# Reordering the warm-up half of an mLSTM + squared-ReLU FFN kernel: early sigmoids, rounding words ahead of exponentials, squares behind num, evenly spread rounding steps

## Chip, cores, metric

One core of one Trainium2 chip. The metric is device time of one execution in microseconds (us), median over several runs. Each run also reports the span of the core (first to last instruction) and the mean clock that TensorE was granted (1.000 is full).

In the text PE is TensorE (matmul), DVE is VectorE, ACT is ScalarE, POOL is GpSimd.

## The reference

```python
# attention part: q,k,v,o_gate (4, 8, 768, 40), i_gate,f_gate (4, 8, 768), all float32
for t in range(S):
    m_new = max(f[t] + m, i[t]);  f_s = exp(f[t] + m - m_new);  i_s = exp(i[t] - m_new);  m = m_new
    C = f_s * C + i_s * outer(v[t], k[t]);   n = f_s * n + i_s * k[t]
    y[t] = sigmoid(o_gate[t]) * (C @ q[t]) / max(|n . q[t]|, 1)
# bridge to x (3072, 320); FFN with w_in (320, 2048), w_out (2048, 320)
out = maximum(x @ w_in, 0)**2 @ w_out
```

The kernel does the recurrence in 24 chunks of 128 steps. The weights arrive as 64-bit words and are rounded to float32 on the chip in 26 pieces.

Of the kernel before, what the change touches and what calls it, by code (L numbers as in the profile page):

```python
# [9 lines left out]
F32 = mybir.dt.float32  # L10
# [3 lines left out]
AF = mybir.ActivationFunctionType  # L14
# [3 lines left out]
P = 128  # L18
# [11 lines left out]
def kernel(  # L30
# [25 lines left out]
    nc = tc.nc  # L56
# [39 lines left out]
    ident = consts.tile([P, P], F32)  # L96
# [158 lines left out]
    st = {}  # L255
# [14 lines left out]
    def load_o(s):  # L270
        b, c = divmod(s, NB)
        r, (s0, s1) = next((r, (a, z)) for r, (a, z) in enumerate(RUNS) if a <= s < z)
        if s == s0:
            st["og", r] = ld.tile([P, 4, H, D], F32, name="og")
        og = st.setdefault(s, {})["og"] = st["og", r][:, s - s0]
        nc.sync.dma_start(og, o_gate[b, :, c * P : (c + 1) * P, :].rearrange("h p d -> p h d"))

    def sigmoid(s):
        nc.scalar.activation(st[s]["og"], st[s]["og"], AF.Sigmoid)

    def load_A(s):
        b, c = divmod(s, NB)
        d = st.setdefault(s, {})
        A = ld.tile([P, H, P], F32, name="A_bc", bufs=2)
        d["A"] = [A]
        nc.sync.dma_start(
            A[:], bass.AP(A_d.tensor, A_d.offset + b * H * S + c * P, [[0, P], [S, H], [1, P]]),
        )
# [19 lines left out]
    def mask(s):  # L308

        A = st[s]["A"][0]  # L310
        nc.gpsimd.affine_select(  # L311
            A[:], A[:], compare_op=ALU.is_ge, fill=-1e30, base=0, pattern=[[0, H], [1, P]], channel_multiplier=-1,
        )

    def weigh(s, masked=False):
        b, c = divmod(s, NB)
        d = st[s]
        A, n = d["A"], H // len(d["A"])
        d["W"] = prep.tile([P, H, P], F32, name="W_sb")
        d["dec"] = prep.tile([P, H], F32, name="dec")  # L320
        if len(A) == 1 and not masked:
            mask(s)
        for i in range(len(A)):
            hh = slice(i * n, (i + 1) * n)
            for h in range(n):
                nc.scalar.activation(  # L326
                    d["W"][:, i * n + h, :], A[i][:, h, :], AF.Exp, bias=b_T[:, b, c, i * n + h : i * n + h + 1],
                )
            nc.scalar.activation(d["dec"][:, hh], A[i][:, :, P - 1], AF.Exp)
        values(s)  # L330
# [37 lines left out]
    def weighted(s, spare=False):  # L368
        d = st[s]
        d["P"] = []  # L370
        for i in range(2):
            t = ffn.tile([P, W], F32, name="r_sb", bufs=4) if spare else work.tile([P, W], F32, name="P_sb")
            t = t[:].rearrange("p (j t) -> p j t", j=PR)
            d["P"].append(t)
            nc.vector.tensor_tensor(  # L375
                t, d["sc"][i], d["W"][:].rearrange("p (j two) t -> p j two t", two=2)[:, :, i, :], op=ALU.mult,
            )

    def attend(s):
        b, c = divmod(s, NB)  # L380
        d = st[s]
        C = st.get("C")
        if c > 0:
            hi = ps_at.tile([P, H, D1], F32, name="hi", tag="at")
            for j in range(PR):
                nc.tensor.matmul(  # L386
                    hi[:, 2 * j : 2 * j + 2, :].rearrange("p h d -> p (h d)"), lhsT=d["qT"][:, j, :],
                    rhs=C[:, j].rearrange("p h d -> p (h d)"), start=True, stop=True,
                )
        if c + 1 < NB:  # L390
            dC = ps_at.tile([P, PR, 2, D1], F32, name="dC", tag="at")
            for j in range(PR):
                nc.tensor.matmul(  # L393
                    dC[:, j].rearrange("p h d -> p (h d)"),
                    lhsT=d["kq"][:, 0, 2 * j : 2 * j + 2, :].rearrange("p h d -> p (h d)"),
                    rhs=d["vw"][:, 2 * j : 2 * j + 2, :].rearrange("p h d -> p (h d)"), start=True, stop=True,
                )
        hp = d["hp"] = ps_at.tile([P, H, D1], F32, name="hp", tag="at")
        for h in range(H):
            nc.tensor.matmul(  # L400
                hp[:, h, :], lhsT=d["P"][h % 2][:, h // 2, :], rhs=d["va"][:, h, :], start=True, stop=True,
            )
        d["num"] = hp
        if c > 0:
            num = d["num"] = work.tile([P, H, D1], F32, name="num", bufs=1)
            nc.vector.tensor_tensor(  # L406
                num[:], hi[:], eA_T[:, b, c, :].unsqueeze(2).to_broadcast([P, H, D1]), op=ALU.mult,
            )
        if c + 1 < NB:
            Cn = work.tile([P, PR, 2, D1], F32, name="C_sb")  # L410
            nc.vector.tensor_tensor(Cn[:], dC[:], bdm[:], op=ALU.mult)  # L411
            if c > 0:
                Cd = work.tile([P, H, D1], F32, name="Cd", bufs=1)
                nc.gpsimd.tensor_tensor(
                    Cd[:], C[:].rearrange("p j i d -> p (j i) d"),
                    d["dec"][:].unsqueeze(2).to_broadcast([P, H, D1]), op=ALU.mult,
                )
                Cf = Cn[:].rearrange("p j i d -> p (j i) d")
                nc.gpsimd.tensor_tensor(Cf, Cf, Cd[:], op=ALU.add)  # L419
            st["C"] = Cn  # L420
# [17 lines left out]
    def turn_rows(s):  # L438
        d = st[s]
        g, j = divmod(s, GT)  # L440
        if j == 0:
            st["xT", g] = xts.tile([P, 3, WG], F32, name="xT")
        tp = ps_at.tile([P, 3, P], F32, name="tp", tag="at")
        for a in range(3):
            nc.tensor.transpose(tp[:, a, :], d["x"][:, a * P : (a + 1) * P], ident[:])  # L445
        nc.scalar.copy(st["xT", g][:, :, j * P : (j + 1) * P], tp[:])
        del st[s]
# [29 lines left out]
    def ffn1(g, pp):  # L477
        ffn1_main(g, pp)
        ffn1_rest(g, pp, st["half"][0])

    def relu_half():
        if "half" in st:
            hs, g4 = st.pop("half")
            rs = []
            for h in hs:
                rs.append(ffn.tile([P, 2, WG], F32, name="r_sb", bufs=4))
                nc.scalar.activation(rs[-1][:], h[:], AF.Relu)  # L487
            st["relu"] = rs, g4

    def square_half():  # L490
        if "relu" in st:
            rs, g4 = st.pop("relu")
            for i, r in enumerate(rs):
                nc.vector.tensor_tensor(g4[:, :, i, :], r[:], r[:], op=ALU.mult)  # L494

# [122 lines left out]
    def idle(n):  # L618
        t = ps_h.tile([P, W], F32, name="idle", tag="h_ps")
        for _ in range(n):  # L620
            nc.tensor.matmul(t[:], lhsT=zeros[:, :P], rhs=zeros[:], start=True, stop=True)
# [43 lines left out]
    weighted(1, spare=True)  # L665
    load(2)
    load_A(2)
    sigmoid(0)
    sigmoid(1)
    attend(0)  # L670
    rounding.step()
    normalise(0)
    load_o(2)
    load_o(3)
    mask(2)
    attend(1)
    normalise(1)
    load(3)
    load_A(3)
    rounding.step()  # L680

    nc.scalar.activation(consts.tile([P, 1], F32, name="warm")[:], ident[:, :1], AF.Exp)
    turn_rows(0)
    idle(4)
    transposes(2)
    idle(4)
    turn_rows(1)
    weigh(2, masked=True)
    rounding.step()


    NEXT = (5, 8, 10, 11, 12, 14, 15, 17, 19, 21, 23, 26)
    assert NEXT[-1] == len(pieces)
    for u in range(8):
        s = 2 + u // 2
        relu_half()
        if u % 2 == 0:
            if u == 0:
                ffn1(0, 0)
                scores(s)  # L700
                rounding.step()
            else:
                turn_rows(s - 1)
                scores(s)
                ffn1(u // 4, u % 4)
            weighted(s)
            weigh(s + 1)
            if u == 2:
                rounding.step()
                rounding.step()  # L710
            square_half()
        else:
            load_A(s + 2)
            for r in {1: (4,), 3: (5, 6), 5: (7,), 7: ()}[u]:
                load(r)
            if u in (1, 5):
                for r in range(s, s + 2 + u // 2):
                    sigmoid(r)
            attend(s)
            rounding.join()  # L720
            normalise(s)
            for r in {5: (8,), 7: (9,)}.get(u, ()):
                load(r)
            if u > 4:
                load_o(2 * s)
                load_o(2 * s + 1)
            transposes(s + 1)
            rounding.words()
            ffn1(u // 4, u % 4)
            square_half()  # L730
        if u < 4:
            load_o(4 + u)
        while rounding.done < NEXT[u]:
            rounding.step()
# [94 lines left out]
```

## The kernel before, where the change touches it

One *piece* of weights is fetched, then `words` (two ScalarE instructions) and `join` (three on VectorE, one add on GpSimd) round it. `step` does the words of the next piece and the join of this one. In the timelines below VectorE, ScalarE and GpSimd each run their own instructions in the order in which the program lists them, so an instruction can be held up by those listed before it on its engine.

The tile names: `hi` and `hp` are the two parts of a chunk's output (from the state carried over, and from within the chunk), `dC` is the chunk's addition to the state `C_sb`, `P_sb` are the weighted scores that `hp` reads, `num` is the sum of both parts, `x_sb` the gated and normalised output. The *turns* are TensorE's transposes of `x_sb`; ScalarE copies them to `xT`, which the first FFN product (`ffn1`) reads together with `w_in`.

```python
def words(self):                                  # ScalarE x2
    nc.scalar.activation(mag[:, :w], raw[:, :, 1].bitcast(F32), AF.Abs)
    nc.scalar.activation(low[:, :w], raw[:, :, 0].bitcast(U32), AF.Copy, bias=2.0, scale=2.0 ** -51)
def join(self):                                   # VectorE x3, GpSimd x1
    nc.vector.tensor_scalar(mag, mag, ...);  nc.vector.tensor_scalar(bits, bits, ...)
    nc.vector.scalar_tensor_tensor(bits, in0=self.raws[n][:, :w, 1], ..., in1=bits, ...)
    nc.gpsimd.tensor_tensor(dst.bitcast(I32), bits, low.bitcast(I32), op=ALU.add)   # dst: w_in or w_out
    self.fetch()                                  # next raw piece, once this buffer is free
...
def weigh(s, masked=False):                       # ScalarE: 8 exponentials; GpSimd: mask, vw
    if len(A) == 1 and not masked: mask(s)        # GpSimd
    ...
def attend(s):                                    # TensorE hi, dC, hp in three PSUM banks (bufs=3)
    ...                                           # VectorE num <- hi, C_sb <- dC; GpSimd Cd, C_sb
def normalise(s):                                 # VectorE: num += hp; dm; x_sb = num * og * dm
    ...
def relu_half(): ...                              # ScalarE: r_sb (bufs=4) <- h_ps
def square_half(): ...                            # VectorE: g <- r_sb * r_sb

# first half: 8 steps u, two for each chunk s = 2..5
NEXT = (5, 8, 10, 11, 12, 14, 15, 17, 19, 21, 23, 26)     # pieces done after each step; last four later
for u in range(8):
    s = 2 + u // 2
    relu_half()
    if u % 2 == 0:
        ...                                       # turn_rows(s-1), scores(s), ffn1
        weighted(s)                               # VectorE: P_sb
        weigh(s + 1)
        if u == 2:
            rounding.step(); rounding.step()
        square_half()
    else:
        ...                                       # loads
        if u in (1, 5): ...                       # sigmoids of the coming chunks
        attend(s); rounding.join(); normalise(s)
        transposes(s + 1); rounding.words(); ffn1(u // 4, u % 4); square_half()
    while rounding.done < NEXT[u]: rounding.step()
```

## Time and profile before

| | before |
|---|---|
| time, median of the first 3 runs | 573.0 us (572.72 to 574.24) |
| profiled execution | span 575.1 us, clock 0.985 |
| busy | PE 98%, DVE 54%, ACT 34%, POOL 17% |

TensorE is nearly always busy, so look for where it is not, and where it runs at half clock. The prediction below shows the lines: three sites, A near 50 us, B near 62 us, C near 132 us.

One line that it used without showing it is VectorE's wait inside site B (timeline of VectorE, before; in brackets the idle time just before and who ended it):

```profile
58.16 0.43 DVE L194 TENSOR_SCALAR mag<-mag 128x512 f32<-128x512 f32 x1 [2.25 <-ACT mag L183]
...
60.65 2.36 DVE L494 TENSOR_TENSOR g<-r_sb 128x512 f32<-128x512 f32 x2
62.93 0.49 DVE L406 TENSOR_TENSOR num<-hi,eA_T 128x328 f32<-128x328 f32 x1
```

VectorE stands still for 2.25 us, until ScalarE has finished the exponentials and made the next magnitude; then join, squares and only then num, for which TensorE waits.

### The profile page before, as it was taken

To read this page: it belongs to the slowest core of one execution; us is meant where nothing else is said; L and a number is where in the kernel's file an instruction comes from. 1 tells how busy PE (TensorE), PEld (TensorE's weight loads), DVE (VectorE), ACT (ScalarE), POOL (GpSimd) and SP (SyncE) were. 2 spreads that over 40 slices of the span, in tenths; PEclk is the share of its full clock that TensorE was granted. 3 is DMA by queue.
4 is the path that set the end of the run, shared out by engine and by line. 5 is a ranking of instruction groups with operands and counts; after the bars stand their busy time and mean duration, and the time that the engine had idled before them with its cause. 6 is when DMAs were issued, how large, how long until landed. Compare 5 with 4: busy or idle time off the path is not lost.

```text
span 575.1 us, 9748 instructions
## 1 busy us (share of the span) xinstructions
PE 562.9 (98%) x3879; PEld 503.8 (88%) x3879; DVE 308.7 (54%) x602; ACT 195.8 (34%) x486; POOL 97.3 (17%) x113
## 2 busy tenths in 40 slices
PE   8998899999999999999999999999999999999997
PEld 5875788887789989989989988988998998988997
DVE  8687867597373364364365356246355454424441
ACT  3868376280442232423213315205126204112000
POOL 3354523233011120100211220101210210000000
PEclk9998799997999999999999999999999999999999
DMA  9996979932132432321441343141321000000000
GB/s 193 229 217 151 151 158 181 179 105 35 59 47 54 90 46 61 83 47 38 84 69 38 62 91 61 27 102 38 47 62 38 0 24 2 1 24 0 25 24 23
DMA packets 130909, 42.60 MB, mean 74 GB/s; under 512 B 101072, under 2 KB 127696, under 8 KB 130864
## 3 DMA queue, kind: packets, MB, share of 16 engines
q1 hardware_dynamic: 130768, 41.79, 35.4%
q8 instruction: 30, 0.49, 0.4%
q10 hardware_dynamic: 96, 0.20, 0.1%
q14 instruction: 15, 0.12, 0.1%
HBM read 37.95 MB, written 4.03 MB: 73 GB/s over the span
## 4 chain that ended last, share of the span: by engine, by line
PE 91%; DVE 5%; ACT 2%; issue 1%; DMA 1%; POOL 0%; SPq 0%; POOLq 0%; ACTq 0%; DVEq 0%
PE h_ps L555 30%; PE h_ps L461 28%; PE h_ps L472 7%; PE hp L400 7%; PE tp L363 4%; PE tp L350 4%; PE dC L393 3%; PE hi L386 3%; PE h_ps L501 3%; DVE mag L198 1%; PE tp L445 1%; DVE g L494 1%; DMA kq<-in_q_dram 1%; ACT W_sb L326 1%; PE A_ps L302 1%
## 5 line engine op out<-in xcount | busy, mean ns | idle before, releaser
L461 PE MATMUL h_ps<-xT,w_in 128*128 128x256 f32 x768 | 180.3, 389 | 2.7 <-POOL w_in L203 2.1
L461 PEld LDWEIGHTS h_ps<-xT,w_in 128*128 128x128 f32 x768 | 144.8, 193 | 26.7 <-issue 3.0
L487 ACT ACTIVATE r_sb<-h_ps 128x512 f32<-128x512 f32 x96 | 49.9, 602 | 176.1 <-PE h_ps L472 170.9
L494 DVE TENSOR_TENSOR g<-r_sb 128x512 f32<-128x512 f32 x96 | 61.3, 698 | 70.3 <-ACT r_sb L487 70.3
L555 PE MATMUL h_ps<-w_out,g 128*128 128x160 f32 x528 | 76.9, 302 | 0.0
L555 PEld LDWEIGHTS h_ps<-w_out,g 128*128 128x128 f32 x528 | 72.5, 190 | 1.3 <-ACT r_sb L487 0.3
L326 ACT ACTIVATE W_sb<-A_bc,b_T 128x128 f32<-128x128 f32 x176 | 53.8, 394 | 6.4 <-POOL A_bc L311 6.4
L555 PE MATMUL h_ps<-T,S 128*128 128x160 f32 x352 | 51.4, 299 | 0.0
L472 PE MATMUL h_ps<-xT,w_in 64*128 64x256 f32 x384 | 49.0, 391 | 0.0
L555 PEld LDWEIGHTS h_ps<-T,S 128*128 128x128 f32 x352 | 49.0, 190 | 0.0
L400 PE MATMUL hp<-va,P_sb 128*128 128x41 f32 x368 | 45.7, 286 | 0.0
L472 PEld LDWEIGHTS h_ps<-xT,w_in 64*128 64x128 f32 x384 | 34.8, 186 | 12.3 <-issue 9.0
L337 POOL TENSOR_TENSOR vw<-va,W_sb 128x328 f32<-128x328 f32 x20 | 16.4, 821 | 169.9 <-ACT W_sb L326 140.4
L400 PEld LDWEIGHTS hp<-va,P_sb 128*128 128x128 f32 x368 | 44.5, 198 | 0.0
L569 DVE TENSOR_TENSOR y_sb<-y_sb,h_ps 128x160 f32<-128x160 f32 x33 | 10.6, 321 | 55.1 <-PE h_ps L555 55.1
L375 DVE TENSOR_TENSOR P_sb<-tp,W_sb 128x512 f32<-128x512 f32 x46 | 29.6, 685 | 16.0 <-PE tp L363 15.5
L419 POOL TENSOR_TENSOR C_sb<-C_sb,Cd 128x328 f32<-128x328 f32 x16 | 14.1, 879 | 140.0 <-DVE C_sb L411 139.9
L569 DVE TENSOR_TENSOR y_sb<-h_ps,y_sb 128x160 f32<-128x160 f32 x22 | 7.1, 325 | 49.5 <-PE h_ps L555 30.9
L350 PE MATMUL tp<-ident,kq 128*128 128x128 f32 x192 | 26.2, 280 | 2.7 <-DVE num L406 2.4
L578 ACT COPY y_sb<-h_ps 128x160 f32<-128x160 f32 x11 | 3.2, 292 | 70.6 <-PE h_ps L555 63.9
L363 PEld LDWEIGHTS tp<-qT,kT 40*128 40x128 f32 x384 | 24.2, 187 | 3.3 <-issue 1.8
L363 PE MATMUL tp<-qT,kT 40*128 40x128 f32 x384 | 26.9, 279 | 0.0
(98 smaller groups left out, 672.1 us busy)
## 6 DMA issues: line engine op xcount, KB each, us to landing
A_bc<-a_rows SPq DMA_DIRECT2D x22, 512.0 KB, 4.3
raw<-in_moe_w_out_dram SPq DMA_DIRECT2D x16, 320.0 KB, 3.3
raw<-in_moe_w_in_dram SPq DMA_DIRECT2D x8, 512.0 KB, 5.5
kq<-in_k_dram SPq DMA_DIRECT2D x24, 160.0 KB, 4.3
kq<-in_q_dram SPq DMA_DIRECT2D x24, 160.0 KB, 4.0
va<-in_v_dram SPq DMA_DIRECT2D x24, 160.0 KB, 4.3
og<-in_o_gate_dram SPq DMA_DIRECT2D x24, 160.0 KB, 4.3
out_dram<-y_sb SPq DMA_DIRECT2D x24, 160.0 KB, 1.8
```

Of the source, the lines that this page charges most:

```text
L326: nc.scalar.activation(d["W"][:, i * n + h, :], A[i][:, h, :], AF.Exp, bias=b_T[:, b, c, i * n + h : i * n + h + 1],)
L350: nc.tensor.transpose(tp[:, j, :], d["kq"][:, i, 2 * j : 2 * j + 2, :].rearrange("p h d -> p (h d)"), ident[:],)
L363: nc.tensor.matmul(sc[i][:, j, :], lhsT=d["kT"][rows, j, :], rhs=d["qT"][rows, j, :], start=True, stop=True,)
L375: nc.vector.tensor_tensor(t, d["sc"][i], d["W"][:].rearrange("p (j two) t -> p j two t", two=2)[:, :, i, :], op=ALU.mult,)
L386: nc.tensor.matmul(hi[:, 2 * j : 2 * j + 2, :].rearrange("p h d -> p (h d)"), lhsT=d["qT"][:, j, :], rhs=C[:, j].rearrange("p h d -> p (h ...
L400: nc.tensor.matmul(hp[:, h, :], lhsT=d["P"][h % 2][:, h // 2, :], rhs=d["va"][:, h, :], start=True, stop=True,)
L461: nc.tensor.matmul(hs[i][:, n, :], lhsT=w_in[:, a, fb * P : (fb + 1) * P], rhs=xT[:, a, :], start=(n == 0 and a == 0), stop=False,)
L472: nc.tensor.matmul(hs[i][:, n, :], lhsT=w_in2[rows, 2 * pp + n, :], rhs=xT[rows, 2, :], start=False, stop=(n == 1),)
L487: nc.scalar.activation(rs[-1][:], h[:], AF.Relu)
L494: nc.vector.tensor_tensor(g4[:, :, i, :], r[:], r[:], op=ALU.mult)
L555: nc.tensor.matmul(to, lhsT=lhsT[:, p], rhs=rhs[:, p, :], start=(start and p == 0), stop=(p == NPAIR - 1), skip_group_check=True,)
L569: add = lambda to, a, b: nc.vector.tensor_tensor(to, a, b, op=ALU.add)
```

## The change

Four parts. (1) The o_gate loads and sigmoids of chunks 2 and 3 move up behind those of chunks 0 and 1, and the one-element `warm` exponential, which loaded the exp table early, is dropped. (2) In step 2 the words of piece 9 come before the exponentials, and the two joins before them too. (3) The squares of that step move into step 3, behind num. (4) `NEXT` gives the steps from the fifth on more pieces and the last one fewer.

```diff
-            st["relu"] = rs, g4
+            st.setdefault("relu", []).append((rs, g4))       # square_half pops the oldest
@@ setup
     load_A(2)
+    load_o(2)
+    load_o(3)
     sigmoid(0)
     sigmoid(1)
@@ (further down: load_o(2), load_o(3) removed)
-    nc.scalar.activation(consts.tile([P, 1], F32, name="warm")[:], ident[:, :1], AF.Exp)
     turn_rows(0)
     idle(4)
     transposes(2)
     idle(4)
+    sigmoid(2)
+    sigmoid(3)
     turn_rows(1)
     weigh(2, masked=True)
@@ steps
-    NEXT = (5, 8, 10, 11, 12, 14, 15, 17, 19, 21, 23, 26)
+    NEXT = (5, 8, 10, 11, 13, 15, 17, 19, 21, 23, 25, 26)
@@ even u
+            if u == 2:
+                rounding.words()
             weighted(s)
-            weigh(s + 1)
             if u == 2:
-                rounding.step()
-                rounding.step()
-            square_half()
+                mask(s + 1)
+                rounding.join()
+                rounding.join()
+                weigh(s + 1, masked=True)
+                rounding.words()
+            else:
+                weigh(s + 1)
+                square_half()
@@ odd u
-            if u in (1, 5):
-                for r in range(s, s + 2 + u // 2):
+            if u == 5:
+                for r in range(4, 8):
                     sigmoid(r)
             attend(s)
+            if u == 3:
+                square_half()
```

## The prediction

> **What bounds the kernel now.** I read the page first. Its parts 1 and 2 say that TensorE sets the time: 98% busy, and the granted clock is full except at the start and in three slices.
>
> ```profile
> PE 562.9 (98%) x3879; PEld 503.8 (88%) x3879; DVE 308.7 (54%) x602; ACT 195.8 (34%) x486; POOL 97.3 (17%) x113
> PE   8998899999999999999999999999999999999997
> PEclk9998799997999999999999999999999999999999
> ```
>
> A slice is 14.4 us, so the dips (8, 7, 7 tenths) lie at 43-58, 58-72 and 129-144 us. From 145 us on nothing is lost; whatever the early part gains should stay in the total. The list of waits of TensorE and its timeline name the gaps.
>
> ```profile
> PE tp L350 <- DVE num L406: 2.4, 1, 2.4
> PE h_ps L461 <- POOL w_in L203: 2.1, 1, 2.1
> PE dC L393 <- DVE P_sb L375: 1.3, 1, 1.3
> ...
> PE tp L445 <- DVE x_sb L435: 0.9, 2, 0.7
> ```
>
> In the timeline the columns are start, us, engine, line, operation:
>
> ```profile
> 51.30 4.98 PE L461 MATMUL h_ps<-xT,w_in 128*128 128x256 f32 x14 [2.08 <-POOL w_in L203]
> 63.47 1.97 PE L350 MATMUL tp<-ident,kq 128*128 128x128 f32 x8 [2.43 <-DVE num L406]
> 133.06 1.10 PE L393 MATMUL dC<-vw,kq 128*128 128x82 f32 x8 [1.35 <-DVE P_sb L375]
> 133.99 3.52 PE L400 MATMUL hp<-va,P_sb 128*128 128x41 f32 x16
> ```
>
> Each gap costs more than its length: the eight transposes after the second take 1.97 us, against 1.07 elsewhere. One-microsecond windows show why (the last columns are granted clock, DMA share and GB/s):
>
> ```profile
> 51.00:52.00 1.00, 0.70 (x3) 0.65 (x4) 0.97 (x2) 0.98 (x2) 0.25 (x1) 1.00 0.84 259
> 53.00:54.00 1.00, 1.00 (x4) 0.82 (x3) 0.97 (x3) 0.00 (x0) 1.00 (x2) 0.50 0.59 82
> ...
> 65.00:66.00 1.00, 1.00 (x5) 0.91 (x4) 0.93 (x4) 0.73 (x3) 0.30 (x1) 0.50 1.19 298
> ...
> 136.00:137.00 1.00, 1.00 (x7) 1.00 (x6) 0.00 (x0) 0.00 (x0) 0.77 (x1) 0.50 1.02 167
> ```
>
> From the fractions at the edges, the clock is half from 52.1 to 55.5 (3.4 us), 62.3 to 69.15 (6.8) and 134.0 to 140.8 (6.8). Half clock for t costs about t/2: 1.7, 3.4 and 3.4 us. So:
> - Site A (46-56 us): 0.65 + 2.08 + 1.7 = 4.4 us.
> - Site B (61-69 us): 2.43 + 3.4 = 5.8 us.
> - Site C (131-141 us): 1.35 + 3.4 = 4.8 us.
> All three: 15 us, 2.6% of 573. That is the ceiling.
>
> **What the Trainium skill says.**
> - "TensorE: Matmul & The Clock Gate", "What's actually happening": activity is judged in windows of 3413 ns, with only half or full clock. The trace agrees: 1.00 and 0.50, lengths 3.4 and 6.8. The page has the drop come after an idle window; here gaps of 1.35 to 2.43 us suffice. The 0.65 us gap at 46.3 did not.
> - "SBUF — State Buffer", "SBUF: two separate sides": VectorE and GpSimd share one port pair as an exclusive lock. The trace agrees: the x_sb product takes 1.17 us at 45.13 and ends 0.34 us after the GpSimd add that began at 44.69, against 0.44 alone.
> - "ScalarE: Activation LUTs", "What ACT_TABLE_LOAD costs": 1283 ns plus a drain of about 1380. The trace has the load at 1.28 us; the next sigmoid follows 0.01 us later, so no drain after it shows here.
>
> **The change, part by part.**
>
> *Sigmoids 2 and 3 early.* This is the view of before around them:
>
> ```profile
> 31.09 2.45 ACT L326 ACTIVATE W_sb<-A_bc,b_T 128x128 f32<-128x128 f32 x8
> 43.34 1.28 ACT L279 ACT_TABLE_LOAD   x1
> 44.63 0.83 ACT L279 ACTIVATE og<-og 128x320 f32<-128x320 f32 x2
> 45.13 1.17 DVE L434 TENSOR_TENSOR x_sb<-num,og 128x320 f32<-128x320 f32 x1 [2.79 <-ACT og L279]
> 49.94 1.31 POOL L203 TENSOR_TENSOR w_in<-mag,low 128x512 int32<-128x512 int32 x1 [3.98 <-ACT low L185]
> ```
>
> The change removes the load and sigmoids at 43.34 (2.1 us), the load at 51.19, the warm-up at 25.1, and VectorE's 2.79 us wait. The sigmoids go into ScalarE's idle time at 29.6-30.4 with their table still active. But without the warm-up the exp load now stands directly before chunk 2's exponentials: load 31.2-32.5, exponentials to 34.95, then the magnitudes that piece 4's rounding on VectorE needs at 35.6, where before they were ready at 34.2. GpSimd's vw (to 35.7) and join 3 (to 36.95) take the lock; piece 4's three VectorE steps end near 38.4 instead of 37.3. P_sb of chunk 2 stands behind them: 38.3 instead of 37.23. The first half ends near 39.0, and dC (38.07 before) needs its bank: a **new gap** of about 1.1 us at 38.
>
> After it everything is 1 us later: mask(3) 39.7, exponentials to 43.3. In before, GpSimd did vw, Cd, C and join 5 (0.74+0.74+0.88+1.27) while VectorE stood idle. Now both want the lock at 43.3-48.6: the GpSimd four (about 3.3 us net of overlap) and VectorE's two products, copy and two squares (about 2.0) alternate. x_sb is ready at 45.4 (before 47.07), so the 0.65 us gap goes; but piece 6's VectorE steps begin at 48.55 (before 48.18) and its GpSimd add ends near 51.6 (before 51.25). TensorE reaches that point at 49.1. The gap at A stays, about 2.5 us, with its half clock. **A: 0.65 + 2.08 becomes 1.1 + 2.5, some 0.4 us worse.**
>
> *Words ahead, squares behind num.* Piece 9's words now precede the exponentials, so VectorE no longer waits 2.25 us for them at 58.16: from 52.5 it runs P_sb (1.3), join 8 (2.4) and join 9 (2.5 with the lock) to 58.7. hi of chunk 3 is ready then, and num runs at 58.75-59.2 instead of 62.93. hp ends near 61.35 and the transposes follow without a wait: B's 2.43 + 3.4 us go. The squares (1.3) are moved, not dropped. They come before x_sb of chunk 3: squares with vw between 60.1-62.0, join 10 with Cd and C to 64.4, the num sum and normalisation with GpSimd's add and mask to 67.9. TensorE, after transposes 0.9 and ffn1 4.6, wants that x_sb at 66.9 and waits about 1 us. Before, it started those turns at 71.78: **71.8 - 68.0 = 3.8 us gained, A's loss and this wait included.**
>
> *Steps spread.* One step with 320 columns costs VectorE 0.32+0.33+0.49 = 1.15 us, 1.7 under the lock. The part before site C had three steps, now it has one; three steps from 127.67 to 132.3 held P_sb until 132.23:
>
> ```profile
> 125.26 2.50 DVE L494 TENSOR_TENSOR g<-r_sb 128x512 f32<-128x512 f32 x4 [0.41 <-ACT r_sb L487]
> 132.23 1.28 DVE L375 TENSOR_TENSOR P_sb<-tp,W_sb 128x512 f32<-128x512 f32 x2
> ```
>
> With one, P_sb starts relative to TensorE at about 129, before hi ends at 131.7; dC need not wait. **4.8 us gained.** The added steps fall in the stretch from 70 to 115 us, where VectorE idles 1.3 to 3.6 us at a time and TensorE never waits; I count them as free. Sum: 3.8 + 4.8 = 8.6 us. For the two new gaps near 1 us I take a chance of about one in three each that the clock halves, at about 2.5 us: 1.6 us. 573 - 8.6 + 1.6 = 566.
>
> **The rivals.**
> 1. *The new gaps are as good as the old ones.* If the exp load before chunk 2 and the late x_sb of chunk 3 both halve the clock (2 x 3.4 us), only 1.8 us is left: 571. For: 1.35 us halved it. Against: the two gaps are shorter, and 0.65 us did not.
> 2. *Site A goes as well.* If the lock alternates less badly, piece 6 lands by 49.5 as the removed wait suggests, and A loses its 2.5 + 1.7 us: 562 or a little less. For: 2.79 us of VectorE's wait do disappear. Against: GpSimd's four operations must still be done there.
> 3. *Only the spread matters*: squares shift B's wait from num to x_sb in full; then C alone gives 4.8 us, 568.
> 4. *Late gates*: if the o_gate of chunks 2 and 3 has not landed by 29.6 (issued near 22 instead of 24.39, median time to land 5.8 us), ScalarE's copy before the first ffn1 is held: up to 1 us more.
>
> **Range and chances.** The sum's best form is 562-564 and rival 1 gives 571; 8 in 10 lie in 561 to 570.5. Faster by over 2% means below 561.5: A must go too, 0.18. Slower by over 2% would need new losses of 20 us: 0.01.
>
> **What would show it right or wrong.** Right: no wait of the chunk 4 transposes on num and none of dC near 130 us, so clock 1.00 there; VectorE no longer waiting on the sigmoids; one exp load before the exponentials at 31; TensorE still waiting on GpSimd's w_in (2 to 2.8 us) near 50, and dC of chunk 2 waiting about 1 us on P_sb. Wrong: no w_in wait (the lock argument fails), half clock right after 38 or 67 us (short gaps count in full), or a new TensorE wait between 70 and 130 us (the spread steps are not free).

## The result

| | before | after |
|---|---|---|
| time, median | 573.16 us (572.72 to 574.24, 4 runs) | 568.49 us (567.82 to 569.93, 4 runs) |
| ratio | | 0.9919, 95% interval 0.9895 to 0.9943 |
| profiled execution | 575.1 us, clock 0.985 | 565.8 us, clock 0.999 |

A ratio is the mean time of one kernel's runs over that of the other's of the same rounds, so not quite the ratio of the medians. The gain is 0.8%, 4.7 us by the medians. The two profiled executions, though, lie 9.3 us apart: twice as much. Keep that in mind.

The page of the kernel after, parts 1 and 2:

```profile
PE 554.9 (98%) x3878; PEld 497.8 (88%) x3879; DVE 312.0 (55%) x602; ACT 193.1 (34%) x483; POOL 98.1 (17%) x113
PEclk9999999999999999999999999999999999999999
```

The clock is full in every slice. TensorE's waits:

```profile
PE tp L445 <- DVE x_sb L435: 3.0, 2, 2.4
PE h_ps L461 <- POOL w_in L203: 1.8, 1, 1.8
...
PE dC L393 <- DVE P_sb L375: 1.1, 1, 1.1
```

The wait of 2.4 us on num is gone. The 1.1 us for dC is not the old one: it stands near 39 us now, as the timeline of TensorE shows:

```profile
39.42 1.09 PE L393 MATMUL dC<-vw,kq 128*128 128x82 f32 x8 [1.08 <-DVE P_sb L375]
51.66 3.29 PE L461 MATMUL h_ps<-xT,w_in 128*128 128x256 f32 x14 [1.77 <-POOL w_in L203]
67.52 0.52 PE L445 MATMUL tp<-ident,x_sb 128*128 128x128 f32 x3 [2.39 <-DVE x_sb L435]
128.00 1.92 PE L400 MATMUL hp<-va,P_sb 128*128 128x41 f32 x16
```

At site C (last line) dC and hp follow without a wait and at full clock: 1.92 us for hp, 3.52 before. At A the fourteen ffn1 matmuls take 3.29 us at full clock, 4.98 before at half clock; but the wait for w_in ends at 51.66, as before (51.30). At B the turns of chunk 3 start at 67.52 instead of 71.78.

Two squares at A, which take 1.29 us together in the profile before (first line), take 1.97 after, and the x_sb product takes 0.92 us (before: 0.49), with GpSimd's vw, Cd, C and rounding add now running at the same time (43.70 to 48.67):

```profile
46.98 1.29 DVE L494 TENSOR_TENSOR g<-r_sb 128x512 f32<-128x512 f32 x2
```
```profile
44.09 0.92 DVE L435 TENSOR_TENSOR x_sb<-x_sb,dm 128x320 f32<-128x320 f32 x1
...
45.57 1.97 DVE L494 TENSOR_TENSOR g<-r_sb 128x512 f32<-128x512 f32 x2
```

VectorE in site B, after:

```profile
58.04 0.69 DVE L199 SCALAR_TENSOR_TENSOR mag<-raw,mag 128x512 int32<-128x512 int32 x1
58.65 0.49 DVE L406 TENSOR_TENSOR num<-hi,eA_T 128x328 f32<-128x328 f32 x1
...
59.47 2.38 DVE L494 TENSOR_TENSOR g<-r_sb 128x512 f32<-128x512 f32 x2
...
66.88 0.49 DVE L435 TENSOR_TENSOR x_sb<-x_sb,dm 128x320 f32<-128x320 f32 x1
```

num is 4.3 us earlier than before, while x_sb of chunk 3, the end of the same queue, is done at 67.6 instead of 68.9. The other part of the 4.3 us by which the turns moved is half clock in the profile of before: there TensorE came to the turns 2.9 us after x_sb was ready, and at full clock (gaps_filled, below) the old order reaches them at 69.43. So at full clock the change gains about 1.9 us at B (an estimate, from one profile of each). Between 31 and 67.5 us VectorE is busy 33.8 of 36.5 us (93%), TensorE 30.7. **In this stretch VectorE is taken to be the bound** (the experiments test it), though TensorE is the busiest engine of the whole span.

### The profile page after: what moved, and what is told of

It is laid out like the page before. It is cut to its first block, busy times and chain, and to the rows that moved or that the text cites. A ratio compares the mean times of both kernels' runs of the same rounds, so it can differ in the third digit from the quotient of the medians.

```text
span 565.8 us, 9740 instructions
## 1 busy us (share of the span) xinstructions
PE 554.9 (98%) x3878; PEld 497.8 (88%) x3879; DVE 312.0 (55%) x602; ACT 193.1 (34%) x483; POOL 98.1 (17%) x113
## 4 chain that ended last, share of the span: by engine, by line
PE 92%; DVE 4%; ACT 1%; issue 1%; DMA 1%; POOL 0%; POOLq 0%; SPq 0%; DVEq 0%
PE h_ps L555 30%; PE h_ps L461 28%; PE h_ps L472 8%; PE hp L400 7%; PE tp L363 4%; PE tp L350 3%; PE h_ps L501 3%; PE dC L393 3%; PE hi L386 3%; PE tp L445 1%; PE idle L621 1%; PE A_ps L302 1%; ACT W_sb L326 1%; DVE mag L198 1%; PE A_ps L298 1%
## 5 line engine op out<-in xcount | busy, mean ns | idle before, releaser
L461 PE MATMUL h_ps<-xT,w_in 128*128 128x256 f32 x768 | 176.7, 383 | 2.3 <-POOL w_in L203 1.8
L461 PEld LDWEIGHTS h_ps<-xT,w_in 128*128 128x128 f32 x768 | 142.2, 190 | 25.1 <-issue 3.0
L487 ACT ACTIVATE r_sb<-h_ps 128x512 f32<-128x512 f32 x96 | 49.9, 601 | 173.8 <-PE h_ps L472 170.6
L400 PE MATMUL hp<-va,P_sb 128*128 128x41 f32 x368 | 44.1, 280 | 0.0
L400 PEld LDWEIGHTS hp<-va,P_sb 128*128 128x128 f32 x368 | 42.9, 192 | 0.0
L446 ACT COPY xT<-tp 128x384 f32<-128x384 f32 x24 | 11.4, 477 | 43.2 <-PE tp L445 43.2
```

Of the source, the lines that this page charges most:

```text
L400: nc.tensor.matmul(hp[:, h, :], lhsT=d["P"][h % 2][:, h // 2, :], rhs=d["va"][:, h, :], start=True, stop=True,)
L461: nc.tensor.matmul(hs[i][:, n, :], lhsT=w_in[:, a, fb * P : (fb + 1) * P], rhs=xT[:, a, :], start=(n == 0 and a == 0), stop=False,)
L487: nc.scalar.activation(rs[-1][:], h[:], AF.Relu)
```

## The experiments

All are correct against the reference. Each was timed in five rounds, with runs of the kernel before beside them. Ratios are to before; where two calls used the same chip, the record pools their runs of before (13 in all for the two calls on one chip, 11 of them already in the first).

| run | median us (range) | ratio (95% interval) | profiled: span, clock |
|---|---|---|---|
| spread_undone | 570.44 (569.63-570.99) | 0.9944 (0.9917-0.9970) | 568.5, 0.993 |
| spread_alone | 571.84 (571.07-572.41) | 0.9970 (0.9943-0.9996) | 569.7, 0.991 |
| sigmoids_undone | 570.29 (567.81-572.79) | 0.9943 (0.9908-0.9978) | 566.3, 0.997 |
| sigmoids_alone | 577.17 (573.45-578.03) | 1.0046 (1.0012-1.0081) | 575.5, 0.985 |
| squares_undone | 569.65 (567.53-570.94) | 0.9918 (0.9884-0.9952) | 569.2, 0.988 |
| gaps_filled | 572.79 (571.21-573.20) | 0.9978 (0.9949-1.0007) | 569.4, 1.000 |
| squares_behind_x | 567.40 (566.51-568.91) | 0.9890 (0.9861-0.9919) | 565.4, 0.994 |
| words_before_first | 568.41 (566.09-570.00) | 0.9902 (0.9868-0.9936) | 564.2, 0.997 |
| words_undone | 572.58 (569.34-573.94) | 0.9960 (0.9921-1.0000) | 570.2, 0.990 |
| step_before_squares | 569.07 (567.27-571.14) | 0.9910 (0.9875-0.9945) | 566.9, 0.991 |
| three_together | 567.47 (564.73-568.96) | 0.9875 (0.9833-0.9917) | 565.6, 0.997 |
| after_again | 569.82 (568.85-571.47) | 0.9927 (0.9893-0.9960) | 569.7, 0.988 |

The intervals are 0.5 to 0.8% wide, that is about 1.5 to 2.4 us to either side. Differences between two runs below about 2 us are therefore not told apart by time, and I then rest on the waits in the traces.

### The spread: undone, and alone

```diff
-    NEXT = (5, 8, 10, 11, 13, 15, 17, 19, 21, 23, 25, 26)
+    NEXT = (5, 8, 10, 11, 12, 14, 15, 17, 19, 21, 23, 26)
```

> The kernel after, with the old list of rounding steps (12, 14, 15, 17, 19, 21, 23, 26). My theory (three VectorE steps held P_sb and with it dC, 1.35 us of wait, plus up to 3.4 us of half clock where the clock drops): the wait of dC on P_sb near 125 us comes back at about 1.3 us; time 1.5 to 4.8 us over the 568.5 of the kernel after, so 570 to 573, a ratio to before of 0.994 to 1.000. Rival, only the spread matters: all of the gain goes, ratio 0.998 to 1.002. Rival, the spread is worth nothing: 0.992.

> The kernel before, with nothing but the new list of steps. My theory: the wait of dC on P_sb near 132 us is gone, the other two sites stay; 1.4 to 4.8 us gained, ratio 0.992 to 0.998. Rival, only the spread matters: ratio 0.992 as the whole change. Rival, worth nothing: 1.000.

Undone, the wait at C is back (spread_undone, timeline of TensorE):

```profile
129.81 1.09 PE L393 MATMUL dC<-vw,kq 128*128 128x82 f32 x8 [1.34 <-DVE P_sb L375]
```

Alone, the dC wait is absent from the list of waits. Time: 2.0 us lost by undoing (570.44 against 568.49; 1.0 to 1.4 us by the ratios to before), 1.2 us gained alone (571.84 against 573.0). So the mechanism is as predicted, but the part is worth 1 to 2 us, near the wait of 1.34, not the 4.8 booked. Neither the "all" nor the "nothing" rival fits. In neither profile does the half clock appear near C, so what half clock there costs was not tested.

### The sigmoids: undone, and alone

The edit on the kernel after; "alone" is the reverse edit on the kernel before.

```diff
-    load_o(2)                     # behind load_A(2);  undone: behind normalise(0)
-    load_o(3)
-    sigmoid(2)                    # before turn_rows(1);  undone: in step 1
-    sigmoid(3)
-            if u == 5: ...        # undone: if u in (1, 5)
+    nc.scalar.activation(consts.tile([P, 1], F32, name="warm")[:], ident[:, :1], AF.Exp)
```

> The kernel after, with the gate loads, the sigmoids of chunks 2 and 3 and the warm-up where they were before. My theory (the early sigmoids only trade one wait for another at site A): the 1.1 us wait of dC near 38 us goes, a wait on x_sb of 0.6 us near 46 and on w_in of about 2 us near 50 are there; time within 1 us of the kernel after, ratio 0.990 to 0.994. Rival, the two removed table loads and the 2.8 us wait of VectorE are the gain: 3 to 4 us slower than after, ratio 0.997 to 0.999.

> The kernel before, with the sigmoids, gate loads and warm-up moved as in the change and nothing else. My theory: VectorE's wait on the sigmoids is gone, but TensorE waits 1 us on P_sb near 38 us and still about 2 us on w_in near 50; ratio 0.998 to 1.002. Rival, the table loads are the gain: 0.993 to 0.995.

The waits are as predicted. Undone: dC near 38 us waits no more, x_sb 0.66 us near 48, w_in 2.09 us. Alone: dC 1.07 us at 39.4, w_in 1.77. The times miss their windows by a little: 0.9943 undone (0.990 to 0.994 was expected; it overlaps the interval of the whole change), and 1.0046 alone, slower than either theory said. Alone, four of six runs had a clock of 0.985 or less, and those took 576.84 to 578.03 us; the other two took 573.45 and 574.05. Why this order meets the half clock more often is not settled. That the two removed table loads (1.28 us each) are the gain is refuted for the kernel before: alone, they gain nothing. Within the whole change this part may be worth about 1 us (0.9943 against 0.9919 and 0.9927), which is inside the noise.

### The squares: put back ahead of num

```diff
                 weigh(s + 1, masked=True)
                 rounding.words()
+                square_half()
...
             attend(s)
-            if u == 3:
-                square_half()
```

> The kernel after, with the squares of the second half put back in front of chunk 3's num. My theory now: VectorE's queue up to x_sb of chunk 3 holds the same work in either order, and that x_sb ends the wait. The transposes of chunk 4 wait 1.5 to 2 us on num again, and the wait of the turns on x_sb falls from 2.4 to about 0.5 us: ratio to before within 0.002 of the whole change's 0.992. Theory of my prediction and of the change's intent (the squares' place is what removes site B): 2 us or more slower than after, ratio 0.995 to 0.999.

0.9918, not told apart from the whole change (0.9919, and 0.9927 in after_again). VectorE and then TensorE in squares_undone:

```profile
59.43 2.36 DVE L494 TENSOR_TENSOR g<-r_sb 128x512 f32<-128x512 f32 x2
61.71 0.49 DVE L406 TENSOR_TENSOR num<-hi,eA_T 128x328 f32<-128x328 f32 x1
...
66.62 1.34 DVE L435 TENSOR_TENSOR x_sb<-x_sb,dm 128x320 f32<-128x320 f32 x1
```
```profile
62.25 1.97 PE L350 MATMUL tp<-ident,kq 128*128 128x128 f32 x8 [1.25 <-DVE num L406]
...
70.78 0.55 PE L445 MATMUL tp<-ident,x_sb 128*128 128x128 f32 x3
```

The wait on num is back (1.25 us, a little under the 1.5 to 2 expected), and VectorE's queue is no longer for it: x_sb is done at 68.2; in the two profiles of the kernel after it is done at 67.6 and 68.3. But in this profile the turns start only at 70.78, because half clock follows the num wait (61.54 to 68.37) and TensorE itself is late; so the trace does not show the expected 0.5 us wait on x_sb, and by itself it doesn't show that the num wait is free. That rests on the time: this profile spans 569.2 us and that of after_again 569.7, both at clock 0.988, and the ratios agree. As far as these go, moving the squares behind num only moved TensorE's wait from one end of VectorE's queue to the other.

### The words: put back behind the exponentials

```diff
-            if u == 2:
-                rounding.words()
             weighted(s)
+            weigh(s + 1)
             if u == 2:
-                mask(s + 1)
-                rounding.join()
-                rounding.join()
-                weigh(s + 1, masked=True)
-                rounding.words()
+                rounding.step()
+                rounding.step()
             else:
-                weigh(s + 1)
                 square_half()
```

> The kernel after, with the third step of the first half as before: chunk 4's exponentials first, then the two whole rounding steps; the squares stay behind num, the spread and the sigmoids stay changed. My theory (the words ahead of the exponentials keep VectorE's queue full, and that queue ends site B): VectorE waits 1.5 to 2.5 us for a magnitude near 57 us again, x_sb of chunk 3 comes that much later, 1.5 to 2.5 us slower than after: ratio to before 0.994 to 0.997. Rival (the place of the squares or the sigmoids make the gain at B): 0.991 to 0.993.

572.58 against 569.82 for after_again: 2.8 us slower by the medians, 1.9 by the means and by the ratios (0.9960 against 0.9927). VectorE and then TensorE in words_undone:

```profile
59.57 0.43 DVE L194 TENSOR_SCALAR mag<-mag 128x512 f32<-128x512 f32 x1 [2.25 <-ACT mag L183]
```
```profile
70.33 0.52 PE L445 MATMUL tp<-ident,x_sb 128*128 128x128 f32 x3 [2.11 <-DVE x_sb L435]
```

The 2.25 us of idle VectorE are back to the digit, and the turns, which wait for x_sb, start at 70.33, 2.16 us later than in after_again (68.17), whose profile has the same half clock near 41 us. This part is what gains at site B. By the medians it is the largest of the change, but its interval overlaps those of the others.

### The clock: filling the gaps of the kernel before

```diff
+                if u == 2: idle(8)        # between scores(3) and the third ffn1 piece
+            if u == 3: idle(9)            # ahead of chunk 4's transposes
+        if s == 7: idle(5)                # between hi and dC in attend
```

`idle(n)` is n matmuls on zeros, which the kernel already used at its start.

> The kernel before, with matmuls on zeros put into its three gaps on TensorE (8 ahead of the first half's third ffn1 piece, 9 ahead of chunk 4's transposes, 5 between hi and dC of chunk 7), nothing else changed. If half clock is a cost of its own on top of the waits: mean clock 0.997 or more in all runs, the spread of the runs under 1 us, and the median 1.5 to 4 us under the kernel before (ratio 0.993 to 0.997), though no wait of another engine is shorter. If the clock is only a symptom, or hidden behind the next wait: 0.998 to 1.003.

The clock came nearly as expected (1.000 in the profile, 0.996 to 0.997 in the others, where 0.997 or more was expected), the time between the two theories: 0.9978, an interval that includes 1. The range was 2.0 us, not under 1. The dummies removed the bad runs (none over 573.2 us; four of the 13 runs of before beside them took over 574) and left the ordinary ones as they were. The trace shows what became of site A's half clock:

```profile
59.59 2.12 PE L623 MATMUL idle<-zeros 128*128 128x512 bf16 x9
63.89 1.09 PE L350 MATMUL tp<-ident,kq 128*128 128x128 f32 x8 [2.18 <-DVE num L408]
...
69.43 0.55 PE L447 MATMUL tp<-ident,x_sb 128*128 128x128 f32 x3
```

TensorE, at full clock since A, reached site B earlier and had 2.12 + 2.18 = 4.3 us to fill until num, against 2.43 in the profile of before; 2.43 + 1.7 is 4.1. num itself came at about the same time. The 1.7 us of half clock at A had been spent inside a wait that was there anyway. The half clock at B was not: the turns start at 69.43 here, 2.35 us earlier than in the profile of before.

### The kernel after, once more

> The kernel after once more, beside the others of this call, for more runs of it. Ratio to before 0.990 to 0.994; the clock of its runs between 0.988 and 0.999, with time following it by about 2 us.

Same program, other draw: span 569.7 at clock 0.988, against 565.8 at 0.999. One-microsecond windows and TensorE's timeline of after_again:

```profile
41.00:42.00 1.00, 1.00 (x7) 1.00 (x6) 0.93 (x4) 0.82 (x3) 0.15 (x1) 0.50 1.11 308
71.00:72.00 1.00, 1.00 (x3) 0.82 (x4) 1.00 (x2) 1.00 (x5) 0.00 (x0) 0.50 1.15 223
```
```profile
52.52 3.72 PE L461 MATMUL h_ps<-xT,w_in 128*128 128x256 f32 x16
68.17 0.76 PE L445 MATMUL tp<-ident,x_sb 128*128 128x128 f32 x3 [1.74 <-DVE x_sb L435]
```

Two stretches at half clock, about 41 to 47.8 and 68.3 to 75.1 us, each after a wait (1.08 us on P_sb, 1.74 us on x_sb). The first is almost free: TensorE comes late enough that the 1.77 us wait on w_in vanishes, and the turns start at 68.17 instead of 67.52. The second has no wait behind it to hide in: an ffn1 group that starts at 145.14 in the first profile starts at 149.03 in this one, 3.9 us later, of which 0.65 were there at 68 us. (The 0.65 need not be the clock's: x_sb itself was ready 0.66 us later in this profile, its product taking 1.26 us instead of 0.49.)

### Three further reorderings

```diff
# squares_behind_x
-            if u == 3:
-                square_half()
             rounding.join()
             normalise(s)
+            if u == 3:
+                square_half()
# words_before_first
-    weigh(2, masked=True)
-    rounding.step()
+    rounding.words()
+    rounding.join()
+    weigh(2, masked=True)
# step_before_squares
             ffn1(u // 4, u % 4)
+            if u == 1:
+                rounding.step()
             square_half()
# three_together: all three
```

> The kernel after, with the early squares of the fourth step put behind the normalisation of chunk 3 instead of between num and the join. My theory (VectorE's queue ahead of x_sb sets the end of site B, the two squares with vw and Cd between them take 2.4 us of it): the wait of the turns on x_sb falls from 2.4 us to under 0.5, 1.5 to 2.4 us faster than after, ratio to before 0.987 to 0.990. Rival, the join and the lock set x_sb, not the squares: ratio 0.992 as after.

> The kernel after, with the words of piece 4 and the join of piece 3 ahead of chunk 2's exponentials. My theory (the exp load that took the warm-up's place delays piece 4's magnitudes, so P_sb of chunk 2 and with it dC): the 1.1 us wait of dC near 38 us is gone, everything up to site B runs 1 us earlier, ratio to before 0.989 to 0.991. Rival, P_sb waits on the exponentials themselves: the dC wait stays at 1 us or more and the ratio is 0.992 or worse.

> The kernel after, with one rounding step of the second step (piece 6's join) ahead of the first half's squares. My theory: piece 6 is ready 1 to 2 us sooner, so the 1.8 us wait on w_in near 50 us goes or falls under 0.7; but VectorE's queue up to chunk 3's x_sb is as long as before, so the wait moves there and the ratio stays at 0.990 to 0.993. Rival, a wait of TensorE that is removed is time gained: 1.5 us or more faster than after, ratio 0.989 or less.

> The kernel after with all three reorderings: piece 4's words and piece 3's join before chunk 2's exponentials, piece 6's join before the first squares, chunk 3's x_sb before the next squares. If VectorE's queue up to x_sb of chunk 3 is what bounds the stretch to 67 us, 1.2 us (no exp load in the way) and 2.4 us (squares behind) come off it and TensorE has no wait over 1 us left: ratio to before 0.982 to 0.986. If the waits only move on to the next chunk: 0.988 to 0.990.

*squares_behind_x*: the wait on x_sb is gone (x_sb is done at 65.5, 2.1 us earlier than in the kernel after), 0.9890 as expected; but TensorE now waits 1.04 us on the copy xT right after. *words_before_first*: the dC wait at 39 us is gone, TensorE's turns of chunk 3 start at 65.88, 1.6 us earlier (0.5 of it already there at 31 us), ratio 0.9902. The dC wait was the work of the exp load that stands ahead of piece 4's magnitudes, as argued: sigmoids_undone, with the warm-up back, ends it too. *step_before_squares*: the wait on w_in is gone from the list and the ratio is 0.9910, as after. Removing that wait of TensorE gave nothing visible in time. Its profile fell on a draw with half clock from 39 to 50 us, so that this trace alone can't say whether the reorder or TensorE's lateness removed the wait; the time is what the verdict rests on.

*three_together* has the lowest ratio, 567.47 us against 569.82 for after_again (runs 564.73 to 568.96 and 568.85 to 571.47), but 0.9875 is short of the 0.982 to 0.986 expected of a queue without new waits (its interval, 0.9833 to 0.9917, reaches into both theories). x_sb of chunk 3 is ready at 64.1, 3.5 us earlier than in the kernel after, and then (ScalarE, TensorE):

```profile
64.81 0.60 ACT L487 ACTIVATE r_sb<-h_ps 128x512 f32<-128x512 f32 x1 [3.97 <-DVE g L494]
66.30 0.60 ACT L487 ACTIVATE r_sb<-h_ps 128x512 f32<-128x512 f32 x1 [0.90 <-DVE g L494]
```
```profile
67.32 5.23 PE L461 MATMUL h_ps<-xT,w_in 128*128 128x256 f32 x16 [1.70 <-ACT xT L446]
```

The postponed squares keep the four r_sb buffers; the next relu waits for them in ScalarE's queue, and the copy xT, which TensorE needs, stands behind that relu. More r_sb buffers would be the next thing to try; it was not tried.

## Why the prediction was right, and where not

566 was predicted, 568.49 measured: inside 561 to 570.5, and "within 2%" as most likely. The number alone proves little: rival 3, which the experiments refute, gave 568, and the hit comes in part from terms booked too high that meet an allowance (1.6 us) that was too low. So the number was partly luck; the waits were not.

**Held, by the traces.**
- Site A stays: w_in was predicted to come near 51.6, it came at 51.66. The reason given, the lock alternating between GpSimd's four operations and VectorE's products, fits the trace after: x_sb's product, copy and squares take 0.92, 0.61 and 1.97 us there, 0.49, 0.20 and 1.29 in the profile before. No run takes GpSimd's operations away, so this is argued and not tested.
- The new dC wait near 38 us: about 1.1 us predicted, 1.08 measured (38.34 to 39.42); words_before_first removes it by taking away its cause.
- The turns of chunk 3 at 68.0: measured 67.52, and num at 58.65 where 58.75 was predicted.
- No wait at C, no new wait between 70 and 130 us: both so.

**Wrong: sums and sizes on the way.**
- At A the prediction's own sum doesn't close: 1.1 + 2.5 less 0.65 + 2.08 is 0.87 us, not 0.4. The 0.4 is the difference of the two times at which w_in is ready. TensorE reached the point at 49.22 in before; with 1.1 added and 0.65 removed that is 49.7, not 49.1. Measured: 49.89, and a wait of 1.77 us, just under the "2 to 2.8" named as a sign of being right, without half clock in this profile.
- The wait of the turns on x_sb was put at about 1 us; it is 2.39 and 1.74 us in the two profiles. x_sb came when predicted, but in the first of them TensorE stood ready at 65.1 instead of 66.9, as A's half clock, booked again, did not occur.
- The chances don't fit each other: 0.18 below 561.5 and 8 in 10 from 561 to 570.5 leave about two in a hundred above 570.5, while two new gaps at one in three each give one in nine for rival 1 at 571.

**Wrong: the half clock booked as certain.** "Half clock for t costs about t/2: 1.7, 3.4 and 3.4 us" came from one profiled execution, at clock 0.985. Of 24 runs of the kernel before whose clock is listed, only five lie there (mean 577.3 us); the other 19 lie at 0.990 to 0.997 (mean 573.1). Each stretch of 3.4 us takes about 0.003 off the mean clock of such a run (1.7 of 570 us), so by this estimate an ordinary run has one to three of them, where the profiled run has five. The 6.8 us at B and C that the change was to save are therefore not lost in full in an ordinary run; where its stretches lie is not recorded. The mis-sized terms are C's 4.8 us, which is 1.2 to 2.0 us in spread_alone and spread_undone, and the 3.4 us of half clock in B's 5.8. In return the kernel after meets the half clock in most of its runs too: ten runs at 0.988 to 0.999, mean 569.5. The 1.6 us allowed for that was too little against 3.9 us in after_again's profile. The means, 574.0 and 569.5, differ by 4.5 us where 7 were predicted.

**Wrong: what gains at B.** The prediction put words and squares into one part and named num's wait as the loss. squares_undone brings that wait back at no cost that the times show; words_undone costs 2.8 us by the medians and 1.9 by the means. The gain is VectorE's 2.25 us of idleness, not the place of the squares.

**The rivals.** 1 (the new gaps halve the clock as the old did) is partly true: in after_again both waits are followed by half clock ("half clock right after 38 or 67 us" was a sign of being wrong), yet the first one is hidden. 2 (A goes too) is refuted. 3 (only the spread matters) is refuted by spread_alone. 4 (late gates) did not happen: the sigmoids start at 29.58 right behind the copies.

**Open.** Which wait halves the clock in a given run, and why sigmoids_alone meets it so often. One thing more is in the clock records of the traces: in all 14 profiles the half clock inside the span starts a whole number of 3.41 us steps after the first full clock and lasts one, two or three steps (before: 52.08, 62.32 and 134.00, 3 and 21 steps apart; after_again: 40.99 and 68.30, 8 apart). Where this grid lies differs by run: the first full clock comes at 4.30 us in before, 6.90 in after_again. So the same wait can fall differently on the grid in two runs. That this decides is not shown: a wait of 1.77 us at 49.9 to 51.7 in after lies wholly inside one step (49.70 to 53.11), and no half clock follows it.

## What to carry to other kernels

Find the engine that bounds the stretch, not the span: where one engine's queue is full, reordering the work ahead of the result that the others need only moves their waits. What helps is taking idle time out of that queue (words_undone, 2.25 us), or putting work behind that result (squares_behind_x, x_sb 2.1 us earlier), until the postponed work holds something else up. A profile is one draw: compare its clock with the clocks of the timed runs before adding up what the throttle costs. And half clock costs only what the next wait for another engine does not cover: of 6.8 us in after_again, at most 0.65 us in one place and 3.2 in another.

## What the Trainium skill lacked or had wrong

- "TensorE: Matmul & The Clock Gate", "What's actually happening": it has half clock follow at least one idle window of about 3.4 us. Here waits of 1.08 us (after_again) and 1.35 us (before) were followed by half clock of 6.8 us, while waits of 1.77 and 2.39 us in the first profile of the kernel after were not. So the length of one wait does not decide it. ("TensorE: Matmul & The Clock Gate", in "A second HAM failure mode: psum-queue depth-cycling", does tell of a clock that oscillates with short idles between groups of matmuls, but gives no length for them.)
- "TensorE: Matmul & The Clock Gate", "Terms": it puts the penalty at the throttled time times one minus the clock's share, which is half of it. Half is not always lost: 6.8 us of half clock put the next chunk off by 0.65 us in one place, where another engine's wait followed, and by 3.2 us (3.9 less 0.65) in another.
- "ScalarE: Activation LUTs", "What ACT_TABLE_LOAD costs": a switch is given as about 2.66 us, 1.38 of it a drain. In the trace of before a load takes 1.28 us and the sigmoid starts 0.01 us after it; no drain is seen after it, nor before it (at 25.12 the load starts 0.02 us after the instruction before it ends). Taking two switches away (sigmoids_alone) gained no time.
- "SBUF — State Buffer", "SBUF: two separate sides": the exclusive lock agrees with the traces. It does not say what happens when both queues stay full: here, at 43.6 to 49 us of the kernel after, the two engines' instructions end in turn, one each with one exception, and two squares that take 1.29 us together alone take 1.97 to 2.38 us.
